# Attention key rests of four heads in one score unit, and a new place for the turns of q, k and X

## The chip, the cores and the metric

One core of a Trainium2 chip runs the whole program. The metric is the time of one execution on the device, in microseconds; smaller is better. The kernel before takes 453.09 us (median of 3 runs, 452.95 to 453.27). The profiled execution has a span of 451.7 us, and all times inside it are counted from the start of that span.

The engines are named as in the profile: PE is TensorE (matmuls), PEld its weight loads, DVE is VectorE, ACT is ScalarE, POOL is GpSimd, SP is SyncE, which here only issues transfers.

## The reference, cut to what matters

```python
def _attn_ref(q, k, v):                      # (8, 12, 448, 64) each: batch, heads, sequence, head width
    scores = (1.0 / np.sqrt(64)) * np.matmul(q, k.transpose(0, 1, 3, 2))
    attn = softmax(scores)                   # over the keys
    return np.matmul(attn, v)

def reference(q, k, v, w_gate, w_val, w_out):
    x = attn_out.transpose(0, 2, 1, 3).reshape(8 * 448, 768)
    g = x @ w_gate                           # 768 x 1536
    val = x @ w_val                          # 768 x 1536
    return (g * sigmoid(g) * val) @ w_out    # 1536 x 768
```

There are 96 heads, which the kernel takes in 48 pairs (two heads of 64 columns fill 128 partitions), six pairs for each of the eight batch entries. The FFN works on eight blocks of 384 or 512 rows of x.

## The kernel before

The parts that the change touches. A pair goes through these steps: q and k are loaded and turned (transposed) to `qkT`; `qk` makes the scores of one group of 112 keys for both heads and ScalarE takes the exponential; `pv_chunk` multiplies the exponentials with the values and with a column of ones, so that the sum of the softmax comes out as column 64; VectorE divides; `turn_x` turns the result into `X`, the moving operand of the FFN.

```python
NPE = 11       # pairs 1 to 10 have q and k turned by TensorE, later ones by a transposing DMA
XPE = 12       # pairs 0 to 11 have X turned by TensorE
FIRST = 6      # pairs worked on before the first FFN step
# ...
    ps_s = ctx.enter_context(tc.tile_pool(name="ps_s", bufs=3, space=PSUM))   # 3 x 2 banks
    ps_f = ctx.enter_context(tc.tile_pool(name="ps_f", bufs=2, space=PSUM))   # 2 banks
# ... in prep(pr), for pairs 1 to 10:
        def turn():
            if pr < FIRST + 2:
                tp = ps_s.tile([128, 2, 1024], FP16, tag="s", name="tp")[:, 0]
            else:
                tp = ps_f.tile([128, 1024], FP16, tag="f", name="tp")
            for i in range(2 * NC + 1):
                t, c = (1 - i // NC, i % NC) if i < 2 * NC else (0, 0)
                for hx in range(2):
                    src = raw[pr][t][:, hx, c, :]
                    nc.tensor.transpose(tp[ts(hx, 64), ts(i, P)], src, ident[0:P, 0:P])
            nc.vector.tensor_copy(qkT[pr][:], tp[:, 0 : 2 * S + D])
# ...
    def qk(pr, c):                                    # c = 0..3: 112 keys each
        t = qkT[pr]
        s = ps_s.tile([128, 2, 512], FP32, tag="s")
        for hx in range(2):
            nc.tensor.matmul(
                s[:, hx, 0:S],
                lhsT=t[ts(hx, 64), c * P : c * P + 128],
                rhs=t[ts(hx, 64), ds(S + (1 - hx) * D, S)],
                start=True, stop=True,
            )
        e = Es[pr % NE][:, ds(c * EB, 16)].rearrange("p (h b) x -> p h (b x)", h=2)
        nc.scalar.activation(e[:, :, 0:S], s[0:P, :, 0:S], AF.Exp, scale=sm_scale)
# ...
    def pv_chunk(pr, c):                              # 8 matmuls of 65 columns; 4 chunks a pair
        if c == 0:
            accs[pr] = ps_f.tile([128, 512], FP32, tag="f", name="acc")      # one bank a pair
        # ... six matmuls of 128 queries of one head, two of the last 64 queries of both heads
        if c < NC - 1:
            return
        nc.vector.reciprocal(r[:, 0:7], a7[:, :, D])
        nc.vector.tensor_tensor(xt[:, 0:n], a7[:, 0:n, 0:D],
                                r[:, 0:n].unsqueeze(2).to_broadcast([128, n, D]), ALU.mult)
# ...
    def turn_x(pr):
        if pr < XPE:
            tp = accs[pr] if pr < FIRST else ps_f.tile([128, 512], FP32, tag="f", name="xtp")
            for j in range(3):
                nc.tensor.matmul(tp[:, ts(j, 128)], lhsT=xt[:, 2 * j : 2 * j + 2].rearrange("p h d -> p (h d)"),
                                 rhs=ident[:], start=True, stop=True)
            nc.vector.tensor_copy(dst[:, 0:MQ], tp[:, 0:MQ])
            return
        # ... else two transposing DMAs
    # turn_rests(b): the last 64 queries of six pairs, 12 matmuls of 64 columns
```

After a start of six pairs the program goes in visits. A visit has two or three score units, up to two products of earlier pairs, and then its share of the first FFN (`gp` and `vp`, six matmuls each) and of the second (`op`, twelve matmuls). The end of a visit in `before`:

```python
            for _, p0 in todo:
                pv(p0)
                if p0 < XPE:
                    turns.append(p0)
                else:
                    turn_x(p0)
            # ... the visit's FFN steps: run_fv(), run_o() ...
            if x == 1:
                turn_rests(0)
            while turns:
                turn_x(turns.pop(0))
```

In the second FFN `op` comes from `ps_f`, ScalarE brings it to `osb`, and the rows are stored. The last 128 rows of all are treated apart, so that their second half is evacuated and stored in two quarters of 192 columns:

```python
        for ch, oh in steps:
            last = last_block and ch == n // 128 - 1
            # ...
            parts = [(oh * OH, OH)]
            if last and oh:
                parts = [(OH, OH // 2), (OH + OH // 2, OH // 2)]
```

Of the kernel before, what the change touches and what calls it, by code (L numbers as in the profile page):

```python
# [19 lines left out]
NPE = 11  # L20
# [3 lines left out]
WIDE = 8  # L24
XPE = 12
NE = 4
NX = 6
NV = 5
VS = 9
EB = 15  # L30
# [3 lines left out]
def kernel(  # L34
# [24 lines left out]
    MQ = S - D  # L59
# [13 lines left out]
    load_table("exp_and_others")  # L73

# [7 lines left out]
    ps_f = ctx.enter_context(tc.tile_pool(name="ps_f", bufs=2, space=PSUM))  # L82

    Es = [consts.tile([P, NC * EB + 1, D], FP16, name=f"E{i}") for i in range(NE)]
    Xts = [consts.tile([128, 7, D], FP16, name=f"xt{i}") for i in range(NX)]
    Xrs = [consts.tile([D, 128], FP16, name=f"xr{i}") for i in range(3)]
    Vts = [consts.tile([P, 2, NC, D + 2], FP16, name=f"vo{i}") for i in range(NV)]
    vraw = consts.tile([P, VS, 2, NC, D], FP16, name="vraw")
# [11 lines left out]
    wo = [consts.tile([128, NFB, OH], FP16, name=f"wo{i}") for i in range(2)]  # L100
# [5 lines left out]
    def dummy(n):  # L106
        wp = ps_f.tile([128, 512], FP32, tag="f", name="wp")
        for _ in range(n):
            nc.tensor.matmul(wp[:], lhsT=warm[:, 0:128], rhs=warm[:], start=True, stop=True)  # L109

    def load_qk32(pr):
        rq = raws.tile([P, 2, NC, D], FP32, tag="rq", bufs=RB)
        rk = raws.tile([P, 2, NC, D], FP32, tag="rk", bufs=RB)
        for dst, src in ((rq, q), (rk, k)):
            nc.sync.dma_start(dst[:], src[0, 2 * pr : 2 * pr + 2].rearrange("h (p c) d -> p h (c d)", c=NC))
        raw[pr] = (rq[:], rk[:])
# [3 lines left out]
    def load_qk16(pr, n=2):  # L120
        h0 = 2 * (pr % 2) if pr >= 14 else 0
        if h0 == 0:
            q16 = raws.tile([P, 4, NC, D], FP16, tag="rq", bufs=RB, name="q16")
            k16 = raws.tile([P, 4, NC, D], FP16, tag="rk", bufs=RB, name="k16")
            pairbuf[:] = [q16, k16]
        q16, k16 = pairbuf
        for dst, src in ((q16, q), (k16, k)):
            flat = src.rearrange("b h s d -> (b h) s d")[2 * pr : 2 * pr + 2 * n]
            nc.gpsimd.dma_start(dst[:, ds(h0, 2 * n)], flat.rearrange("h (p c) d -> p h (c d)", c=NC))  # L129
        for i in range(n):  # L130
            h = h0 + 2 * i
            raw[pr + i] = (q16[:, h : h + 2], k16[:, h : h + 2])

    def load_v(pr, n=1):
        b, h = divmod(2 * pr, H)
        nc.gpsimd.dma_start(  # L136
            vraw[:, ds(pr % VS, n)].rearrange("p r h c d -> p (r h) (c d)"),
            v[b, h : h + 2 * n].rearrange("h (p c) d -> p h (c d)", c=NC),
        )
# [4 lines left out]
    def load_w(kind, i):  # L144
        if kind == "o":
            src = moe_w_out[:, ts(i, OH)].rearrange("(f p) m -> p f m", p=128)
            dst = wo[i]
        else:
            src = (moe_w_gate if kind == "g" else moe_w_val)[:, ts(i, DF // 4)].rearrange(
                "(t a p) m -> t p a m", p=128, t=2  # L150
            )
            for t in range(2):
                nc.gpsimd.dma_start(wgv[kind, i][:, ts(t, NCB // 2), :], src[t])
            return
        nc.gpsimd.dma_start(dst[:], src)

    def prep(pr):
        rq, rk = raw[pr]
        if pr == 0 or pr >= NPE:
            qk16 = attp.tile([P, 2, NC, 2, D], FP16, tag="qk16", bufs=3)  # L160
            for t, src in enumerate((rq, rk)):
                dst = qk16[:, 1 - t].rearrange("p c h d -> p h c d")
                if pr == 0:
                    nc.vector.tensor_copy(dst[:, 0], src[:, 0])
                    nc.scalar.activation(dst[:, 1], src[:, 1], AF.Copy)
                else:
                    nc.gpsimd.tensor_copy(dst, src)  # L167
        qkT[pr] = attp.tile([128, 2 * S + D], FP16, tag="qkT", name="qkT", bufs=5)
        if pr >= NPE:
            nc.sync.dma_start_transpose(  # L170
                qkT[pr][:, 0 : 2 * S].rearrange("p (c q) -> p c q", q=P),
                qk16[:].rearrange("p t c h d -> p (t c h d)"),
            )
            nc.sync.dma_start_transpose(
                qkT[pr][:, 2 * S :].rearrange("p (c q) -> p c q", c=1),
                qk16[0:D, 1, 0].rearrange("p h d -> p (h d)"),
            )
            return None

        def turn0():  # L180
            for t in range(2):
                tp = ps_s.tile([128, 2, 512], FP32, tag="s", name="tp")
                for c in range(NC):
                    for hx in range(2):
                        nc.tensor.matmul(
                            tp[ts(hx, 64), c // 2, ds(c % 2 * P, P)],
                            lhsT=qk16[:, 1 - t, c, hx],
                            rhs=ident[0:P, 0:P],
                            start=True,
                            stop=True,  # L190
                        )
                dst = qkT[pr][:, ts(1 - t, S)].rearrange("p (a x) -> p a x", a=2)
                nc.vector.tensor_copy(dst[:, 0], tp[:, 0, 0 : 2 * P])
                nc.scalar.activation(dst[:, 1], tp[:, 1, 0 : 2 * P], AF.Copy)
                if t == 0:
                    tq = tp
            nc.vector.tensor_copy(qkT[pr][:, 2 * S :], tq[:, 0, 0:D])

        def turn():
            if pr < FIRST + 2:  # L200
                tp = ps_s.tile([128, 2, 1024], FP16, tag="s", name="tp")[:, 0]
            else:
                tp = ps_f.tile([128, 1024], FP16, tag="f", name="tp")
            for i in range(2 * NC + 1):
                t, c = (1 - i // NC, i % NC) if i < 2 * NC else (0, 0)
                for hx in range(2):
                    src = raw[pr][t][:, hx, c, :]
                    nc.tensor.transpose(tp[ts(hx, 64), ts(i, P)], src, ident[0:P, 0:P])  # L208
            nc.vector.tensor_copy(qkT[pr][:], tp[:, 0 : 2 * S + D])  # L209

        return turn if pr else turn0

    def qk(pr, c):
        t = qkT[pr]
        s = ps_s.tile([128, 2, 512], FP32, tag="s")
        for hx in range(2):
            nc.tensor.matmul(  # L217
                s[:, hx, 0:S],
                lhsT=t[ts(hx, 64), c * P : c * P + 128],
                rhs=t[ts(hx, 64), ds(S + (1 - hx) * D, S)],  # L220
                start=True,
                stop=True,
            )
        e = Es[pr % NE][:, ds(c * EB, 16)].rearrange("p (h b) x -> p h (b x)", h=2)
        nc.scalar.activation(e[:, :, 0:S], s[0:P, :, 0:S], AF.Exp, scale=sm_scale)  # L225

    def qk_half(pr, half, between=None):
        for c in (2 * half, 2 * half + 1):
            qk(pr, c)
            if between and c % 2 == 0:  # L230
                between()
# [3 lines left out]
    def pv_chunk(pr, c):  # L235
        if c == 0:
            accs[pr] = ps_f.tile([128, 512], FP32, tag="f", name="acc")
        e = Es[pr % NE]
        vo = Vts[pr % NV]
        a7 = accs[pr][:, 0 : 7 * (D + 1)].rearrange("p (s d) -> p s d", s=7)  # L240
        for j in range(3):
            for hx in range(2):
                nc.tensor.matmul(  # L243
                    a7[:, 2 * j + hx],
                    lhsT=e[:, ds(c * EB + 9 * hx + 2 * j, 2)].rearrange("p b x -> p (b x)"),
                    rhs=vo[:, hx, c, 0 : D + 1],
                    start=c + j + hx == 0,
                    stop=False,
                )
        for hx in range(2):  # L250
            nc.tensor.matmul(  # L251
                a7[:, 6],
                lhsT=e[:, ds(c * EB + 6 + hx, 2)].rearrange("p b x -> p (b x)"),
                rhs=vo[:, hx, c, 0 : D + 1],
                start=False,
                stop=c == NC - 1 and hx == 1,
            )
        if c < NC - 1:
            return
        r = attp.tile([128, 8], FP32, tag="R", bufs=2, name="R")  # L260
        xt = Xts[pr % NX]
        nc.vector.reciprocal(r[:, 0:7], a7[:, :, D])  # L262
        n = 7 if pr < XPE else 6
        nc.vector.tensor_tensor(  # L264
            xt[:, 0:n],
            a7[:, 0:n, 0:D],
            r[:, 0:n].unsqueeze(2).to_broadcast([128, n, D]),
            ALU.mult,
# [373 lines left out]
```

The softmax here doesn't subtract the row's maximum and nothing guards it: scores larger than these inputs give would overflow.

## Time and profile before

| | us |
|---|---|
| median time of 3 runs | 453.09 |
| span of the profiled execution | 451.7 |
| exponentials on ACT, 192 | 162.1 busy, 919 ns each |
| products of both kinds on PE, 1536 matmuls | 53.0 and 42.9 busy |
| scores on PE, 384 matmuls | 50.6 busy |
| first FFN on PE, 1152 matmuls | 124.7 and 124.6 busy |
| second FFN on PE, 684 matmuls | 116.1 busy |
| first FFN step of the first block starts at | 29.8 |
| last FFN block's first step starts at | 393.8 |

Matmuls overlap in their pipeline, and the recorded length of one counts its whole way through the array. So the busy times of the groups add up to more than the engine's own, and the price of a matmul is better read from the distance between two starts. The granted clock of TensorE is full in all 40 slices of the profile.

In a timeline a line gives the start, the length, the engine, the line of the kernel, the operation, what it writes and reads, its shape, how many are merged, and in brackets how long the engine was idle before it and who released it.

### The profile page before, as it was taken

To read this page: it belongs to the slowest core of one execution; us is meant where nothing else is said; L and a number is where in the kernel's file an instruction comes from. 1 tells how busy PE (TensorE), PEld (TensorE's weight loads), DVE (VectorE), ACT (ScalarE), POOL (GpSimd) and SP (SyncE) were. 2 spreads that over 40 slices of the span, in tenths; PEclk is the share of its full clock that TensorE was granted. 3 is DMA by queue.
4 is the path that set the end of the run, shared out by engine and by line. 5 is a ranking of instruction groups with operands and counts; after the bars stand their busy time and mean duration, and the time that the engine had idled before them with its cause. 6 is when DMAs were issued, how large, how long until landed. Compare 5 with 4: busy or idle time off the path is not lost.

```text
span 451.7 us, 9871 instructions
## 1 busy us (share of the span) xinstructions
PE 441.9 (98%) x4024; PEld 247.0 (55%) x4024; DVE 201.6 (45%) x447; ACT 238.8 (53%) x350; POOL 141.8 (31%) x228
## 2 busy tenths in 40 slices
PE   8999999999999999999999999999999999999995
PEld 3655565545455556454555656545455666544563
DVE  3666562456654434455443534353453544055300
ACT  6965666566746465554554546644555462222221
POOL 8755715927642225252313405330100000000000
PEclk9999999999999999999999999999999999999999
DMA  9999999999969379874749758772503112200033
GB/s 142 173 200 201 196 172 174 180 209 119 145 93 133 46 129 124 132 120 71 126 74 120 98 78 143 118 105 68 101 20 68 46 46 57 70 2 0 17 100 95
DMA packets 105101, 48.71 MB, mean 108 GB/s; under 512 B 59744, under 2 KB 101600, under 8 KB 105056
## 3 DMA queue, kind: packets, MB, share of 16 engines
q0 software_dynamic: 43392, 23.37, 41.2%
q1 hardware_dynamic: 61664, 24.71, 28.9%
q8 instruction: 31, 0.51, 0.5%
q14 instruction: 14, 0.11, 0.1%
HBM read 47.19 MB, written 11.01 MB: 129 GB/s over the span
## 4 chain that ended last, share of the span: by engine, by line
PE 93%; DVE 3%; ACT 2%; issue 1%; DVEq 0%; ACTq 0%
PE op L371 24%; PE gp L326 23%; PE vp L326 23%; PE s L217 9%; PE acc L243 9%; PE acc L251 2%; ACT E L225 2%; PE tp L208 1%; PE wp L109 1%; DVE t L345 1%; ACT sg L341 1%; DVE qkT L209 0%; DVE xt L264 0%; PE acc L291 0%; DVE hts L348 0%
## 5 line engine op out<-in xcount | busy, mean ns | idle before, releaser
L225 ACT ACTIVATE E<-s 112x896 f16<-112x896 f32 x192 | 162.1, 919 | 27.5 <-PE s L217 27.4
L326 PE MATMUL gp<-X,wg 128*128 128x384 f16 (+1 forms) x576 | 124.7, 352 | 0.0
L326 PE MATMUL vp<-X,wv 128*128 128x384 f16 (+1 forms) x576 | 124.6, 352 | 0.0
L371 PE MATMUL op<-wo,hts 128*128 128x384 f16 (+1 forms) x684 | 116.1, 323 | 0.0
L345 DVE SCALAR_TENSOR_TENSOR t<-sg,gp 128x384 f32<-128x384 f32 (+1 forms) x96 | 59.7, 621 | 121.8 <-ACT sg L341 121.8
L341 ACT ACTIVATE sg<-gp 128x384 f32<-128x384 f32 (+1 forms) x96 | 52.5, 547 | 84.8 <-PE gp L326 83.6
L371 PEld LDWEIGHTS <-hts 128*128 128x128 f16 x684 | 65.5, 98 | 45.9 <-issue 3.9
L326 PEld LDWEIGHTS <-wv 128*128 128x128 f16 x576 | 56.3, 98 | 52.6
L326 PEld LDWEIGHTS <-wg 128*128 128x128 f16 x576 | 53.1, 97 | 45.6 <-issue 1.1
L378 ACT ACTIVATE osb<-op 128x384 f32<-128x384 f32 (+1 forms) x57 | 27.8, 487 | 92.5 <-PE op L371 92.5
L167 POOL COPY qk<-q 112x512 f16<-112x512 f16 x37 | 22.9, 619 | 144.5 <-DMA qkT<-qk 143.1
L348 DVE SCALAR_TENSOR_TENSOR hts<-t,vp 128x384 f16<-128x384 f32 (+1 forms) x96 | 59.6, 621 | 10.0
L243 PEld LDWEIGHTS <-E 112*128 112x128 f16 x1152 | 46.7, 97 | 18.2 <-issue 17.5
L243 PE MATMUL acc<-vo,E 112*128 112x65 f16 x1152 | 53.0, 193 | 1.3 <-DVE vo L142 0.7
L217 PE MATMUL s<-qkT 64*128 64x448 f16 x384 | 50.6, 355 | 0.2
L251 PE MATMUL acc<-vo,E 112*128 112x65 f16 x384 | 42.9, 193 | 0.0
L262 DVE RECIPROCAL R<-acc 128x7 f32<-128x7 f32 x48 | 9.8, 205 | 70.6 <-PE acc L251 70.5
L129 POOL DMA_DIRECT2D k<-in_k_dram x44 | 29.0, 660 | 9.5 <-DMA wo<-in_moe_w_out_dram 7.8
L129 POOL DMA_DIRECT2D q<-in_q_dram x44 | 29.3, 666 | 5.2 <-PE s L217 2.5
L136 POOL DMA_DIRECT2D vraw<-in_v_dram x42 | 28.0, 666 | 8.4 <-DVE vo L142 7.2
L217 PEld LDWEIGHTS <-qkT 64*128 64x128 f16 x384 | 14.5, 94 | 25.8 <-issue 18.6
L264 DVE TENSOR_TENSOR xt<-acc,R 128x384 f16<-128x384 f32 (+1 forms) x48 | 27.6, 574 | 1.7
(41 smaller groups left out, 148.2 us busy)
## 6 DMA issues: line engine op xcount, KB each, us to landing
q<-in_q_dram POOLq DMA_DIRECT2D x41, 112.0 KB, 4.0
k<-in_k_dram POOLq DMA_DIRECT2D x41, 112.0 KB, 4.6
vraw<-in_v_dram POOLq DMA_DIRECT2D x39, 112.0 KB, 4.6
wg<-in_moe_w_gate_dram POOLq DMA_DIRECT2D x8, 288.0 KB, 10.1
wv<-in_moe_w_val_dram POOLq DMA_DIRECT2D x8, 288.0 KB, 10.2
wo<-in_moe_w_out_dram POOLq DMA_DIRECT2D x2, 1152.0 KB, 22.0
out_dram<-osb SPq DMA_DIRECT2D x8, 288.0 KB, 3.0
out_dram<-osb SPq DMA_DIRECT2D x8, 240.0 KB, 3.1
```

Of the source, the lines that this page charges most:

```text
L129: nc.gpsimd.dma_start(dst[:, ds(h0, 2 * n)], flat.rearrange("h (p c) d -> p h (c d)", c=NC))
L136: nc.gpsimd.dma_start(vraw[:, ds(pr % VS, n)].rearrange("p r h c d -> p (r h) (c d)"), v[b, h : h + 2 * n].rearrange("h (p c) d -> p h (c ...
L217: nc.tensor.matmul(s[:, hx, 0:S], lhsT=t[ts(hx, 64), c * P : c * P + 128], rhs=t[ts(hx, 64), ds(S + (1 - hx) * D, S)], start=True, stop=True,)
L225: nc.scalar.activation(e[:, :, 0:S], s[0:P, :, 0:S], AF.Exp, scale=sm_scale)
L243: nc.tensor.matmul(a7[:, 2 * j + hx], lhsT=e[:, ds(c * EB + 9 * hx + 2 * j, 2)].rearrange("p b x -> p (b x)"), rhs=vo[:, hx, c, 0 : D + 1] ...
L251: nc.tensor.matmul(a7[:, 6], lhsT=e[:, ds(c * EB + 6 + hx, 2)].rearrange("p b x -> p (b x)"), rhs=vo[:, hx, c, 0 : D + 1], start=False, st ...
L326: nc.tensor.matmul(dst[:, 0:n], lhsT=wslice(kind, fb, cb), rhs=X[kk][:, cb, ds(c0, n)], start=(cb == 0), stop=(cb == NCB - 1),)
L341: nc.scalar.activation(sg[:, 0:n], gp[:, 0:n], AF.Tanh, scale=0.5)
L345: nc.vector.scalar_tensor_tensor(t1[:, 0:n], sg[:, 0:n], 1.0, gp[:, 0:n], ALU.add, ALU.mult)
L348: nc.vector.scalar_tensor_tensor(hts[:, fb, 0:n], t1[:, 0:n], 0.5 * HS, vp[:, 0:n], ALU.mult, ALU.mult)
L371: nc.tensor.matmul(op[:, 0:w], lhsT=hts[:, fb, ts(ch, 128)], rhs=wo[oh][:, fb, ds(m0 - oh * OH, w)], start=(fb == 0), stop=(fb == NFB - 1),)
L378: nc.scalar.activation(osb[:, ds(m0, w)], op[:, 0:w], AF.Copy, scale=1.0 / HS)
```

## The change

Three things are changed, and much follows from them.

**Key rests shared by four heads.** The 448 keys of a head are taken as three groups of 128 and a rest of 64, instead of four groups of 112. The rests of two heads of each of two neighbouring pairs make one score unit: four matmuls of 64 x 64 tiles, two above each other in one PSUM tile. So two pairs have seven units and seven exponentials, where they had eight. To have the rows at the right partitions, values, and the keys of the pairs that the DMA turns, are loaded in two halves of 64 partitions; the key in the middle of each seven is loaded into both.

**More turns by TensorE.** `NPE` goes from 11 to 14 and `XPE` from 12 to 18. The turn of X now takes all 448 queries of a pair at once, so `turn_rests` goes away.

**Order.** The start follows a written list (`START`), and the turns move: in visits with no product the turn of q and k comes behind the first FFN step; in visits with one, the turns come before the FFN steps.

```diff
-NPE = 11
+NPE = 14
-XPE = 12
+XPE = 18
-NX = 6
+NX = 3
+NR = 3
...
     def qk(pr, c):
-        t = qkT[pr]
         s = ps_s.tile([128, 2, 512], FP32, tag="s")
-        for hx in range(2):
-            nc.tensor.matmul(
-                s[:, hx, 0:S],
-                lhsT=t[ts(hx, 64), c * P : c * P + 128],
-                rhs=t[ts(hx, 64), ds(S + (1 - hx) * D, S)],
...
+        if c < KR:
+            t = qkT[pr]
+            for hx in range(2):
+                nc.tensor.matmul(
+                    s[:, hx, 0:S],
+                    lhsT=t[ts(hx, 64), ts(c + low(pr, hx), 128)],
+                    rhs=t[ts(hx, 64), ds(NC * 128, S)],
...
+        else:
+            for hx in range(2):
+                for p in (pr, pr + 1):
+                    lo = low(p, hx)
+                    t = qkT[p]
+                    nc.tensor.matmul(
+                        s[ts(1 - lo, 64), hx, 0:S],
+                        lhsT=t[ts(hx, 64), ds(0 if lo else KR * 128 + 64, 64)],
+                        rhs=t[ts(hx, 64), ds(NC * 128, S)],
...
+    def pv_open(pr):
+        if pr not in accs:
+            if wide(pr):                     # pairs 0 to 5 and the last two
...
+            else:
+                accs[pr] = ([fbank(), fbank()], [0, 0])
+
+    def pv_close(pr):
...
+        for hx in range(2):
+            a4 = accs[pr][0][hx][:, 0 : (KR + 1) * (D + 1)].rearrange("p (s d) -> p s d", s=KR + 1)
+            r = attp.tile([128, KR + 1], FP32, tag="R", bufs=4, name="R")
+            nc.vector.reciprocal(r[:], a4[:, :, D])
+            nc.vector.tensor_tensor(
+                xt[:, :, hx],
+                a4[:, :, 0:D],
+                r[:].unsqueeze(2).to_broadcast([128, KR + 1, D]),
+                ALU.mult,
             )
 
-    def pv(pr):
-        for c in range(NC):
-            pv_chunk(pr, c)
+    def pv(pr, mid):
+        for hx in range(2):
+            for c in range(KR):
+                pv_piece(pr, c, (hx,))
+            if hx == 0:
+                mid()
+        pv_close(pr)
...
         if pr < XPE:
-            tp = accs[pr] if pr < FIRST else ps_f.tile([128, 512], FP32, tag="f", name="xtp")
-            for j in range(3):
+            tp = ps_s.tile([128, 2, 512], FP32, tag="s", name="xtp")[:, 0]
+            for j in range(KR + 1):
+                n = min(128, S - j * 128)
...
                 while l < l0 + 128:                              # second FFN, the stores
                     b, j = divmod(l, S)
-                    c, p0 = divmod((j + D) % S, P)
-                    m = min(P - p0, l0 + 128 - l, (MQ if j < MQ else S) - j)
+                    n = S // NC
+                    c, p0 = divmod(j, n)
+                    m = min(n - p0, l0 + 128 - l)
...
             for _, p0 in todo:
-                pv(p0)
+                pv(p0, run_turns)
                 if p0 < XPE:
                     turns.append(p0)
                 else:
...
+            def between():
+                run_turns()
+                if x + 7 < NPE:
+                    prep(x + 7)()
+
+            if not bare:
+                between()
+            if steps:
+                nf, no = steps.pop(0)
...
+                gate_small[0] = bare
                 for y in range(nf):
-                    if fvq:
-                        run_fv()
+                    run_fv()
+                    if bare and y == 0:
+                        between()
                 for _ in range(no):
                     run_o()
-            if x == 1:
-                turn_rests(0)
-            while turns:
-                turn_x(turns.pop(0))
```

A visit now has three score units in every case but the first (whose two already stand in the start's list) and the last, and at most one product. The eight rest matmuls of a product (`pv_piece(p0, RU)`) come directly behind the visit's scores. The second FFN of the first block moves from its own visits to those of the second block. `w_out` is loaded in four pieces instead of two, later.

## Prediction

> **What bounds the kernel now.** I read the page's busy table first, then the chain that ended last, then TensorE's timeline in a settled stretch and in the two places where it waits.
>
> ```profile
> PE 441.9 (98%) x4024; PEld 247.0 (55%) x4024; DVE 201.6 (45%) x447; ACT 238.8 (53%) x350; POOL 141.8 (31%) x228
> PE 93%; DVE 3%; ACT 2%; issue 1%; DVEq 0%; ACTq 0%
> ```
>
> TensorE is busy for 441.9 of 451.7 us and the chain of work is 93% TensorE. All else is half idle. So time is won by taking TensorE work away, and lost wherever TensorE waits inside its own order of instructions; ScalarE time matters only in the start, where 26 exponentials of 0.84 us stand close together between 6.6 and 29.3 us.
>
> TensorE's timeline of one settled stretch (start us, length us, what, count) gives the price of each kind of work:
>
> ```profile
> 157.63 0.74 PE L217 MATMUL s<-qkT 64*128 64x448 f16 x6
> 158.31 0.35 PE L243 MATMUL acc<-vo,E 112*128 112x65 f16 x6
> ...
> 159.28 1.14 PE L326 MATMUL gp<-X,wg 128*128 128x384 f16 x6
> 160.26 1.14 PE L326 MATMUL vp<-X,wv 128*128 128x384 f16 x6
> 161.23 2.11 PE L371 MATMUL op<-wo,hts 128*128 128x384 f16 x12
> 163.28 0.74 PE L217 MATMUL s<-qkT 64*128 64x448 f16 x6
> 163.95 0.34 PE L371 MATMUL op<-wo,hts 128*128 128x384 f16 x1
> ```
>
> Read start to start. Twelve second-FFN matmuls take 1.95 us, 162.5 ns each. The next scores start 0.10 us after them (161.23 + 1.95 = 163.18, start 163.28). Three score units (two heads each) take 0.67 us; two took 0.48 us in another visit (33.78 to 34.26), so one unit is 0.19 us and a batch pays 0.10 us on each side. The product of one pair with its values (32 matmuls) takes 159.28 - 158.31 = 0.97 us, 30.3 ns each.
>
> Two other rows are needed: two column halves at work together, and the one place where TensorE waits for a softmax division.
>
> ```profile
> 37.15 0.38 PE L310 MATMUL rtp<-ident,xt 128*64 128x64 f16 x12 [0.19 <-DVE t L345]
> 37.46 0.55 PE L217 MATMUL s<-qkT 64*128 64x448 f16 x4
> ```
>
> Twelve matmuls of 64 columns, alternating between two halves of the array, fill 0.38 us; a single one lasts 0.197 us, so 11 steps took 0.18 us, 16.6 ns each.
>
> ```profile
> 28.43 0.22 PE L251 MATMUL acc<-vo,E 112*128 112x65 f16 x2
> 28.68 0.21 DVE L262 RECIPROCAL R<-acc 128x7 f32<-128x7 f32 x1 [0.17 <-PE acc L251]
> 28.93 0.63 DVE L264 TENSOR_TENSOR xt<-acc,R 128x448 f16<-128x448 f32 x1
> 29.61 0.34 PE L291 MATMUL acc<-ident,xt 128*128 128x128 f16 x3 [0.96 <-DVE xt L264]
> ```
>
> When the turn of X follows its own product with nothing between, TensorE idles 0.96 us behind reciprocal and multiplication. Counted from where the next matmul could have started (28.43 + 2 x 0.030 = 28.49) it loses 1.12 us. Before, this happens at the end of the start only; later, X is turned at the end of a visit, after the FFN steps.
>
> **What the Trainium skill says.** "TensorEngine Tiling (Array Packing)", Key Properties: a change of tiling mode drains TensorE, while tiles of one mode run independently. The trace agrees: 0.10 us on each side of a batch of half-height scores, and 16.6 ns per matmul for two halves. "PSUM — Partial Sum Buffer", Engine vs sequencer instructions: matmuls start and complete in program order, only weight loads are pulled ahead. The trace agrees at 29.61 us, where FFN matmuls ready to run stay behind the waiting turn. "TensorE: Matmul & The Clock Gate", Back-to-back issue gap: N/2.4 + 2.5 ns; 384 columns give 162.5 ns, exactly the row above.
>
> **The change, part by part.** The FFN stays at 327 us (576 x 162.5 ns, 576 x 216 ns, 56 x 1.95 us).
>
> A. Scores. 192 units become 168: three of 128 keys per pair and one rest unit per two pairs. After the start, before has 168 units in 58 batches: 168 x 0.19 + 58 x 0.20 = 43.5 us. After has 145 in 49 batches: 27.6 + 9.8 = 37.4 us; in 21 batches the rest unit (64 x 64 tiles) stands beside whole ones and adds a mode change of 0.10, 2.1 us. This holds if the four rest matmuls share the array. Saved: 4.0 us.
>
> B. Products. The 8 rest matmuls of a pair use half the rows each and alternate. At 16.6 ns instead of 30.3 a pair costs 24 x 30.3 + 8 x 16.6 = 0.86 us instead of 0.97. 42 pairs after the start: 4.6 us saved.
>
> C. Turns of q and k by TensorE. In the visits pairs 7 to 13 instead of 8 to 10. One was 0.57 us (34.26 to 34.83) and about 0.1 of switching, three make 2.0 us. One is now 16 small (16.6 ns), 8 of 112 columns (25 ns) and three mode changes, 0.27 + 0.20 + 0.30 = 0.77 us, seven make 5.4 us. Added: 3.4 us.
>
> D. Turns of X. Six of 0.18 us and two rest turns of 0.4, 1.9 us, become twelve of 0.21 us (pairs 6 to 17): 2.5 us. Added: 0.6 us.
>
> E. The start. 23 exponentials stand before the first FFN step instead of 26, which is 2.5 us of ScalarE. TensorE has about 20 us of work there, so it becomes nearly the limit itself, with only one accumulator. I take 2 us saved.
>
> So far this is 8.6 us of saving in A and B, 4.0 spent in C and D, 2 more saved: 6.6 us faster, near 446.5.
>
> F. Where X's turn stands. In a visit with a product, after.py puts the pair into `turns` after `pv`, and `between()` empties that list directly after, ahead of the FFN step. The hook in the middle of `pv` always finds an empty list. Twelve times the turn thus follows its own division at once. The two heads are closed one after the other, each from its own bank. Twelve matmuls (0.36 us) lie between the end of head 0 and of head 1. From the rows of 128x384 (557 ns) and 128x448 (625 ns) a multiplication of 256 columns is 0.42 us. With T the end of head 1: head 0's reciprocal (0.20) and multiplication start at T - 0.32 and end, with 0.03 between instructions, at T + 0.33; head 1's follow and end at T + 1.01; the turn starts at T + 1.06. T lies 0.16 after the place where the next matmul could have started, so each costs 1.22 us. Twelve: 14.6 us.
>
> G. Both FFN banks. The product now holds both banks of the pool it shares with the second FFN operand and the second FFN. Where a visit ends with a first-FFN step, VectorE must finish `hts` first: 0.9 us after the step's last matmul, against the 0.77 us that three scores give. About 11 visits, some 0.2 us each: 2 us.
>
> H. The end. The inner loop of the second FFN now assigns `n = S // NC`, so `last` is never true again: the last rows are not halved. The last evacuation is 0.49 us instead of 0.33, and the last store is 336 KB (4.2 us to landing in the table of transfers) instead of 48 KB (2.0 us). About 2 us.
>
> Sum: -6.6 + 14.6 + 2 + 2 = +12 us, 465. Before already idles 2.7 us between 29.8 and 86.6 us (56.8 us long, 54.1 us of work by the prices above), some of which the new waits will cover, and E and H are rough. I choose 463.
>
> **Rivals.** (1) The saving wins: if VectorE's chain were hidden, about 449 with G and H. For it speak the 98% and the fewer instructions; against it the order itself, in which nothing stands between product and turn. (2) The rest units gain nothing, because their four matmuls run two at a time (21 x 0.19 = 4 us more) and rest products stay at 30 ns (4.6 us more): about 471. Against it speak the 16.6 ns of the two column halves; no row of before shows four quarters at work. (3) Loads become the bound: GpSimd issues keys and values in two halves (0.66 us an issue, some 76 more, 50 us), with a seventh of the rows read twice. GpSimd is busy only 31%, and in before the last gate and value weights are issued at 38.8 us and land within 11.8 us, well ahead of need. A late load in the start could cost 2 to 3 us, about 466.
>
> **Range and chances.** The work left for TensorE cannot give 2%: even with E in full and none of F, G, H the time stays near 446, above the 444.0 that this needs. Faster by over 2%: 0.03. The border to slower by over 2% is 462.2. F is the large term, 12 waits of 1.0 to 1.3 us; with 1.0, and the savings somewhat better, 457 comes out; with rival 2 in part, 469. Hence 454 to 469, within 2%: 0.40, slower: 0.57.
>
> **What would show it.** TensorE's matmuls `xtp<-ident,xt` waiting for `xt` some 12 us in all in the table of waits, 12 times, right after a product; score units of 0.19 us including the rest unit; 0.86 us from the first rest product to the next kind of work; the first FFN step near 27.5 us; about 7 us instead of 5 between the last matmul and the end. I am wrong if those waits are short, if FFN steps lie between product and turn, or if a TensorE wait on a transfer appears.

## Result and the profile after

| | before | after |
|---|---|---|
| median time, us | 453.18 | 466.66 |
| lowest to highest | 452.95 to 454.66 | 466.41 to 468.08 |
| span of the profiled execution | 451.7 | 464.8 |
| first FFN step starts at | 29.79 | 26.62 |
| first step of the last FFN block starts at | 393.8 | 407.0 |

The changed kernel is slower: ratio 1.0297, 95% interval 1.0267 to 1.0327. The predicted time was 463.0, the range 454 to 469.

The busy table and the chain of work of the changed kernel, to be set beside those of before:

```profile
PE 441.9 (95%) x4163; PEld 248.1 (53%) x4163; DVE 206.5 (44%) x464; ACT 219.9 (47%) x325; POOL 178.7 (38%) x298
PE 87%; DVE 6%; ACT 5%; issue 1%; DVEq 0%; ACTq 0%
```

TensorE is busy for exactly as long as before, 441.9 us, in a span that is 13.1 us longer. ScalarE lost 19 us of work and nothing came of it. In the chain the share of TensorE falls from 93% to 87%, VectorE takes 6% instead of 3% and ScalarE 5% instead of 2%: the chain now passes through divisions, copies and exponentials for which TensorE stands still. The equal busy times do not say that no work was saved: the recorded length of a matmul runs on into the wait behind it, so a wait of 1.08 us from start to start shows as 0.92 us of idle time, and most of the short waits below show as none.

The table of waits of the changed kernel (engine, line, what it waited for, us in total, times, the longest):

```profile
PEld L364 <- DVE xt L337: 12.5, 12, 1.0
PE xtp L364 <- DVE xt L337: 8.3, 9, 0.9
PE s L256 <- DVE qkT L247: 2.3, 2, 1.2
PE f L291 <- DVE hts L410: 1.2, 6, 0.2
```

The first row is the one to read: the weight load of X's turn waits for the division, 12 times and 12.5 us in all. The second row has nine of the same waits again on the matmul side; in the three others the exponential on the PSUM slot ended 0.04 to 0.05 us later by this profile, and the wait is put down to it. Rows three and four are two smaller waits.

One visit of the changed kernel, its timeline without weight loads and GpSimd:

```profile
46.73 0.74 PE L256 MATMUL s<-qkT 64*128 64x448 f16 x6
47.04 0.55 DVE L410 SCALAR_TENSOR_TENSOR hts<-t,f 128x384 f16<-128x384 f32 x1
47.14 2.54 ACT L277 ACTIVATE E<-s 128x896 f16<-128x896 f32 x3 [0.79 <-PE s L256]
47.31 0.19 PE L291 MATMUL f<-vo,er 64*128 64x65 f16 x1
47.52 0.29 DVE L168 COPY vo<-vraw 128x512 f16<-128x512 f16 x1
47.65 0.28 PE L291 MATMUL f<-vo,er 64*128 64x65 f16 x7
47.86 0.91 PE L291 MATMUL f<-vo,E 128*128 128x65 f16 x24
48.44 0.18 DVE L336 RECIPROCAL R<-f 128x4 f32<-128x4 f32 x1 [0.64 <-PE f L291]
48.66 0.42 DVE L337 TENSOR_TENSOR xt<-f,R 128x256 f16<-128x256 f32 x1
49.00 0.17 DVE L336 RECIPROCAL R<-f 128x4 f32<-128x4 f32 x1
49.21 0.42 DVE L337 TENSOR_TENSOR xt<-f,R 128x256 f16<-128x256 f32 x1
49.69 0.37 PE L364 MATMUL xtp<-ident,xt 128*128 128x128 f16 x4 [0.92 <-ACT E L277]
```

The product's 24 full matmuls start at 47.86 and need 0.73 us; the turn starts at 49.69, 1.83 us later. Between them VectorE does four instructions, head 0 and then head 1, as the prediction drew it. In the last line the wait is put down to an exponential, which ended at 49.68; the second multiply ended at 49.63, so without the exponential the turn would have started 0.05 us earlier at most. And at the top, one of the eight rest matmuls runs at 47.31 and the other seven start 0.34 us later, when `hts` has ended at 47.59: the second FFN bank was not free.

The start-to-start distances between the first FFN step and the last FFN block, summed by the kind of matmul that opens each stretch (a wait is counted with the kind in front of it):

| us | before | after | of it waits |
|---|---|---|---|
| scores | 38.80 | 34.87 | 3.1 |
| rest products | - | 14.28 | 5.4 |
| products | 40.88 | 44.09 | 13.0 |
| turns of q and k | 1.70 | 4.80 | |
| turns of X | 2.68 | 2.86 | |
| first FFN, gate | 93.52 | 93.56 | |
| first FFN, value | 96.08 | 95.38 | |
| second FFN | 90.34 | 90.53 | |
| sum | 364.00 | 380.37 | 21.5 |

Without its waits the changed kernel would do scores and products in 71.7 us where before takes 79.7. The two kinds have to be taken together: the switch from half-height to full-height matmuls stands behind the scores in before and behind the rest products in the changed kernel.

### The profile page after: what moved, and what is told of

Its sections match the earlier page's. It is cut to its first block, busy times and chain, and to the rows that moved or that the text cites. A ratio compares the mean times of both kernels' runs of the same rounds, so it can differ in the third digit from the quotient of the medians.

```text
span 464.8 us, 10196 instructions
## 1 busy us (share of the span) xinstructions
PE 441.9 (95%) x4163; PEld 248.1 (53%) x4163; DVE 206.5 (44%) x464; ACT 219.9 (47%) x325; POOL 178.7 (38%) x298
## 3 DMA queue, kind: packets, MB, share of 16 engines
q1 hardware_dynamic: 54800, 23.06, 26.8%
## 4 chain that ended last, share of the span: by engine, by line
PE 87%; DVE 6%; ACT 5%; issue 1%; DVEq 0%; ACTq 0%
PE f L433 24%; PE f L388 23%; PE gp L388 21%; PE f L291 8%; PE s L256 5%; ACT E L277 3%; DVE xt L337 2%; PE s L269 2%; PE acc L291 1%; DVE t L407 1%; DVE hts L410 1%; ACT sg L403 1%; PE xtp L364 1%; PE tp L246 1%; PE wp L117 1%
## 5 line engine op out<-in xcount | busy, mean ns | idle before, releaser
L277 ACT ACTIVATE E<-s 128x896 f16<-128x896 f32 x144 | 123.1, 924 | 11.8 <-PE s L256 11.5
L388 PE MATMUL f<-X,wv 128*128 128x384 f16 (+1 forms) x576 | 124.6, 352 | 0.0
L433 PE MATMUL f<-wo,hts 128*128 128x384 f16 x672 | 115.5, 326 | 0.0
L388 PE MATMUL gp<-X,wg 128*128 128x512 f16 (+1 forms) x522 | 113.5, 354 | 0.0
L440 ACT ACTIVATE osb<-f 128x384 f32<-128x384 f32 x56 | 27.5, 491 | 107.0 <-PE f L433 102.8
L410 DVE SCALAR_TENSOR_TENSOR hts<-t,f 128x384 f16<-128x384 f32 (+1 forms) x96 | 59.6, 621 | 10.0
L124 POOL DMA_DIRECT2D vraw<-in_v_dram x82 | 51.1, 653 | 3.9 <-DVE hts L410 1.2
L291 PEld LDWEIGHTS <-E 128*128 128x128 f16 x1152 | 37.8, 97 | 3.9 <-issue 1.2
L291 PE MATMUL f<-vo,E 128*128 128x65 f16 x960 | 36.2, 193 | 0.0
L337 DVE TENSOR_TENSOR xt<-f,R 128x256 f16<-128x256 f32 x80 | 34.0, 424 | 2.8
```

What stands on the lines that cost most here:

```text
L124: eng.dma_start(dst[ts(s, 64)], rows)
L277: nc.scalar.activation(e[:, 0 : 2 * S].rearrange("p (h q) -> p h q", h=2), s[:, :, 0:S], AF.Exp, scale=sm_scale)
L291: nc.tensor.matmul(accs[pr][0][hx][:, ts(j, D + 1)], lhsT=e[rows, ds(hx * S + j * 128, 128)], rhs=Vts[pr % NV][rows, hx, col, 0 : D + 1], ...
L337: nc.vector.tensor_tensor(xt[:, :, hx], a4[:, :, 0:D], r[:].unsqueeze(2).to_broadcast([128, KR + 1, D]), ALU.mult,)
L388: nc.tensor.matmul(dst[:, 0:n], lhsT=wslice(kind, fb, cb), rhs=X[kk][:, cb, ds(c0, n)], start=(cb == 0), stop=(cb == NCB - 1),)
L410: nc.vector.scalar_tensor_tensor(hts[:, fb, 0:n], t1[:, 0:n], 0.5 * HS, vp[:, 0:n], ALU.mult, ALU.mult)
```

## Experiments

**1. X turned in the next visit.** The theory: the twelve waits behind the division are the loss. The rival: TensorE would wait a little later for the same engines.

```diff
             def between():
-                run_turns()
+                if bare:
+                    run_turns()
```

> After, with the turn of X of pairs 6 to 17 moved out of its own visit: it runs in the middle of the next visit's product, or behind the first FFN step where the next visit has no product. Nothing else changes. Theory (the twelve waits of 1.09 us behind the division are the loss): the rows xtp<-ident,xt no longer wait for xt, 13 us less minus 0.1 us each for the PSUM slot of the first score unit, so about 454.5. Rival (TensorE would wait for the same things a little later, in the FFN step, because ScalarE and VectorE are behind): under 4 us less, 463 or more.

Measured: 455.76 us, ratio to before 1.0051 (1.0032 to 1.0069). TensorE's timeline of this run, the same visit:

```profile
45.97 0.54 PE L291 MATMUL f<-vo,E 128*128 128x65 f16 x12
46.35 0.36 PE L364 MATMUL xtp<-ident,xt 128*128 128x128 f16 x4
46.55 0.53 PE L291 MATMUL f<-vo,E 128*128 128x65 f16 x12
```

The turn now stands between the two heads of the next product, and 0.38 us after the first 12 matmuls it runs, with no wait. In the sums by kind the products fall from 44.09 to 32.98 us. The median is 10.9 us under that of the changed kernel, and the span of the profiled execution 11.1 us, where the waits were 13.0: they are gone, but a product with the turn in its middle takes 0.80 to 0.89 us in eight visits and 1.15 and 1.21 us in two, against 0.74 us for one without, and so 1.9 us come back. The rival falls.

**2. The same wait put into the kernel before.** If the placement alone does it, before must show it too.

```diff
                 pv(p0)
-                if p0 < XPE:
-                    turns.append(p0)
-                else:
-                    turn_x(p0)
+                turn_x(p0)
```

> Before, with one thing of the change done alone: X of pairs 6 to 11 is turned directly behind its own product instead of at the end of the visit. Theory: six waits of 0.96 us idle, 1.12 us from start to start, so 6.7 us more, about 459.8. Rival (before has slack elsewhere that takes the wait in): under 2 us more.

Measured: 459.35 us, ratio 1.0127 (1.0095 to 1.0159), 5.7 us more than the 453.64 of before, measured beside it. Its timeline and its table of waits:

```profile
38.61 0.22 PE L251 MATMUL acc<-vo,E 112*128 112x65 f16 x2
39.78 0.34 PE L291 MATMUL xtp<-ident,xt 128*128 128x128 f16 x3 [0.96 <-DVE xt L264]
39.97 1.14 PE L326 MATMUL gp<-X,wg 128*128 128x384 f16 x6
```

```profile
PE xtp L291 <- DVE xt L264: 5.7, 6, 1.0
```

Six turns, six waits of 0.96 us idle. The wait does not need the rest units or the two banks; it comes from the place alone. In the sums by kind the products take 6.8 us more, as expected; the turns of X take 1.0 us less, which is why the time grows by 5.7 and not by 6.7 us.

**3. The turn of q and k before the FFN step everywhere.** Two waits that the prediction did not have: scores wait for the copy of `qkT`. TensorE and VectorE in the changed kernel:

```profile
33.09 0.44 PE L246 MATMUL tp<-ident,k 64*64 64x64 f16 x16
33.78 0.55 PE L256 MATMUL s<-qkT 64*128 64x448 f16 x4
34.28 0.56 DVE L410 SCALAR_TENSOR_TENSOR hts<-t,f 128x384 f16<-128x384 f32 x1
34.75 0.65 DVE L247 COPY qkT<-tp 128x960 f16<-128x960 f16 x1
35.45 0.36 PE L256 MATMUL s<-qkT 64*128 64x448 f16 x2 [1.13 <-DVE qkT L247]
```

Behind the FFN step the turn stands directly before the next visit's scores. Its copy comes after `hts` on VectorE, and the third score unit reads it.

```diff
-            if not bare:
-                between()
+            between()
...
                 for y in range(nf):
                     run_fv()
-                    if bare and y == 0:
-                        between()
```

> After, with the turn of q and k placed before the first FFN step in the visits without a product too. Theory (scores wait 0.5, 1.29 and 1.31 us for the copy of qkT at 29.4, 33.8 and 62.3 us, because the turn now stands directly before the scores that read it): these waits go, 3 us less, about 463.5. Rival (the placement was right, the copy of qkT would then delay hts and the FFN step): no change or up to 1 us more.

Measured: 465.29 us, ratio 1.0247 (1.0215 to 1.0279). The rows for `qkT` leave the table of waits, and the median falls by 1.4 us of the 3 expected. Between the first FFN step and the last block 2.3 us are saved: the scores take 2.2 us less and the rest products 0.6 us more, and one turn of 0.7 us now stands in front of the first FFN step and so outside this stretch. That step starts 1.2 us later than in the changed kernel's profile, 0.8 us for the turn and 0.4 us because in this profile the whole start runs later (first scores at 6.74 instead of 6.32). The theory names the wait rightly, and less than half of its size comes out.

**4. The last 128 rows.** Step H of the prediction said that the lost halving costs 2 us.

```diff
-                    n = S // NC
-                    c, p0 = divmod(j, n)
-                    m = min(n - p0, l0 + 128 - l)
+                    rows_ = S // NC
+                    c, p0 = divmod(j, rows_)
+                    m = min(rows_ - p0, l0 + 128 - l)
```

> After, with the inner variable of the store loop given another name, so that the last 128 rows are again evacuated and stored in two quarters at the end. The prediction's step H says 2 us less (464.7). Rival: the end after the last matmul is as long in after (5.25 us from the last start to the end of the span) as in before (5.28), so the size of the last store costs nothing there: under 0.5 us of change.

Measured: 465.27 us, ratio 1.025 (1.0221 to 1.0278). From the first matmul of the last second-FFN stretch to the end of the span it takes 25.1 us, against 26.7 in the changed kernel: 1.6 us less. So here the halving is worth nearly what H said. But the same distance in before, which has the halving, is 26.8 us: the rival's premise (two ends of equal length) is as true as H's gain. The traces show what differs. Before stores each of the last quarters as 64 rows and 64 rows, all issued by SyncE, which takes 0.55 to 0.60 us for each of these issues. The last evacuation ends at 446.92, the last store is issued 1.3 us later, at 448.26, and lands at 450.26. In this run the quarters go out as 112 rows from SyncE and 16 from ScalarE; the last two are issued at 460.94 and 460.95, right after the evacuation's end at 460.92, and have landed at 462.86. This is read from the traces; a version of before with its stores on two engines was not run.

**5. The three edits together.**

> After with three edits together: X turned in the next visit, the turn of q and k before the first FFN step in all visits, the last 128 rows stored in two quarters. Theory (the three causes lie one after the other on TensorE's path and add up): 455.8 with the first alone, 1.1 less and 1.6 less by the spans of the other two, so 453, level with before (ratio 0.998 to 1.002). Rival (they overlap, or the moved turns get in each other's way): 455 or more.

Measured: 454.5 us, ratio 1.003 (1.0014 to 1.0047), between the two expectations. TensorE's timeline and the table of waits show a wait that had not been seen before, but for 0.17 us in experiment 1:

```profile
68.75 0.55 PE L256 MATMUL s<-qkT 64*128 64x448 f16 x4
71.32 0.36 PE L256 MATMUL s<-qkT 64*128 64x448 f16 x2 [2.01 <-DMA qkT<-qk]
```

```profile
PE s L256 <- DMA qkT<-qk: 2.0, 1, 2.0
PE xtp L364 <- ACT er L277: 1.1, 2, 0.6
```

With the waits gone TensorE arrives earlier than the first `qkT` that the transposing DMA makes, which lands at 71.18 us. In the changed kernel it landed at 69.93, and the same scores ran at 76.01 only: the waits for the division had covered this transfer. And X's turn in front of the FFN step waits 0.56 us for its PSUM slot.

**6. X by the transposing DMA.** Would it not be simplest to leave these turns to the DMA, as before does from pair 12?

```diff
-XPE = 18
+XPE = 6
```
(on top of the edits of 3 and 4; with XPE = 6 the edit of 1 has no turn left to move)

> After with the turn of q and k before the FFN step and the last rows in two quarters, and with X of pairs 6 to 17 turned by the transposing DMA (XPE = 6) instead of TensorE. Theory (each turn of X by TensorE costs 1.09 us of waiting and 0.2 us of work): twelve turns less, 15.5 us less than after with the same two edits (464), so 448.5 to 451. Rival (TensorE's turns were there because the transposing DMA comes too late while the weights are loading): FFN steps wait for X, 455 or more.

Measured: 465.54 us, ratio 1.0261 (1.0247 to 1.0275). The rival holds. The table of waits:

```profile
PE gp L388 <- DMA X<-xt: 7.4, 2, 3.7
PE s L256 <- DVE vo L168: 4.5, 1, 4.5
```

Two FFN steps wait 3.7 us each for a transposed X. The 4.5 us of the second row stand before the scores that waited in experiment 5. The row names a value copy, but scores do not read values; the transposed `qkT` of this pair lands at 71.94 and the scores start at 72.08, the same 0.14 us later as in experiment 5 (71.18 and 71.32). So it is the transposing DMA there too. So at this stage the turns by TensorE do have a use; only their place was bad.

**7. Pairs 12 and 13 by the DMA again**, on top of the three edits (`NPE = 12`).

> The three edits, with pairs 12 and 13 turned by the transposing DMA again (NPE = 12). Theory (a turn of q and k costs TensorE 0.7 us and nothing is won): 1.4 us less than the three edits. Rival (the transposing DMA is late at this place, with the weights under way): scores wait on a transfer for qkT and it takes 1 us or more longer.

Measured: 458.64 us, ratio 1.0099 (1.0078 to 1.012), 4.1 us more than the three edits. TensorE's timeline:

```profile
58.29 0.56 PE L256 MATMUL s<-qkT 64*128 64x448 f16 x4 [1.47 <-DMA qkT<-qk]
71.66 0.56 PE L256 MATMUL s<-qkT 64*128 64x448 f16 x2 [3.22 <-DMA qkT<-qk]
```

4.7 us of waiting for two transposed `qkT`, where the profile of the three edits has 2.0, against 1.5 us of turns saved. This part of the change is right for this stage.

**8. Rest products between the heads**, on top of the three edits, where the visit before ended with a first-FFN step.

```diff
             if hx == 0:
                 mid()
+                if late:
+                    pv_piece(pr, RU)
```

> The three edits, and in visits that follow a first-FFN step the eight rest matmuls of the product stand between the two heads instead of in front of both. Theory (in some 13 visits the rest matmuls wait 0.2 to 0.4 us for the FFN bank that hts still reads, because they need both banks at once): those waits go, 0.35 us each, for 0.1 us more of mode change, so 3 us less than the three edits alone. Rival (the wait only moves to the next user of the banks): within 1 us of the three edits.

Measured: 455.05 us, ratio 1.0034 (1.002 to 1.0048), no gain. The rest products fall from 14.64 to 10.22 us in the sums by kind, so the wait for `hts` is what stood in them. But products rise by 1.9, scores by 1.35 and turns of X by 0.6 us: half-height and full-height matmuls now alternate more often (the 12 matmuls in front of the rest products take 0.47 instead of 0.38 us), the scores have the switch behind them again, and the turn of X comes earlier and waits five times for its PSUM slot, 0.8 us in all. Nearly all is given back.

**9. w_out later**, on top of the three edits.

```diff
-            9: [("o", 0), ("o", 1)],
-            11: [("o", 2), ("o", 3)],
+            12: [("o", 0)],
+            13: [("o", 1)],
+            14: [("o", 2)],
+            15: [("o", 3)],
```

> The three edits, with the four pieces of w_out loaded when pairs 12, 13, 14 and 15 are entered instead of two each at 9 and 11. Theory (with the waits gone TensorE reaches the scores of the first pair turned by the transposing DMA before its qkT has landed, a 2.0 us wait at 71.3 us, and that landing is slow because 2.3 MB of w_out stand before it): the wait goes, 2 us less than the three edits, about 452.5. Rival (the loads of q and k themselves are late): the wait stays, 454.5.

Measured: 453.67 us, ratio 1.0003 (0.9995 to 1.0011). At the place of the 2.01 us wait TensorE's timeline now reads:

```profile
68.65 0.74 PE L256 MATMUL s<-qkT 64*128 64x448 f16 x6
69.23 0.19 PE L291 MATMUL f<-vo,er 64*128 64x65 f16 x1
```

The wait is gone. The two transfers of this pair land in 4.5 and 5.2 us, where they took 8.7 and 11.0 us in experiment 5; they are also issued 1.5 to 2 us earlier. So it was the load of w_out beside them. The median gains 0.8 us where 2 were expected; the three edits' profiled execution, with its 2.0 us, was one of the longer ones of that kernel (457.1 against a median of 454.5), so the wait was probably smaller in most.

**10. X behind the FFN step again in visits with no product**, on top of 9.

> As the one with w_out later, and in visits with no product the turn of X stands behind the first FFN step again (only the turn of q and k stays in front). Theory (in front it waits 0.56 us for an exponential to free its PSUM slot, in three visits): 1 us to 1.5 us less than the one with w_out later, about 451.3, under before by 0.5%. Rival: the slot wait only moves to the next FFN step, no change.

Measured: 453.1 us, ratio 0.9991 (0.9976 to 1.0005): 0.6 us less, level with before. The 1.1 us of waiting for an exponential leave X's turn; a turn of q and k in front of an FFN step keeps two waits of 0.55 us, and the scores behind the FFN step get a new one of 0.7 us. So part of the wait has only moved, as the rival said, and half of the gain expected comes out.

**11. XPE = 12**, on top of 10.

> As the one with X behind the FFN step, with X of pairs 12 to 17 turned by the transposing DMA (XPE = 12). Theory (in time, now that w_out no longer loads at 60 us but still loads at 80 to 100): six turns of 0.2 to 0.3 us less, about 450. Rival (w_out now collides with these transposes): FFN steps wait for X, 453 or more.

Measured: 451.14 us, ratio 0.9949 (0.9937 to 0.9961): under both kernels. Its table of waits has no row of TensorE waiting for a transfer of X or of `qkT`. The turns of X cost 1.28 us instead of 2.45 in the sums, and the products 31.84 instead of 33.02. Pairs 12 to 17 reach the FFN late enough for the DMA; pairs 6 to 11 did not in experiment 6, with w_out in its first place, and were not tried with w_out later.

It is worth a look where the 2.3 us come from by which its profiled span is shorter than that of before: 2.2 from the start, 1.2 from the end, while between the first FFN step and the last block it takes 1.1 us more than before (365.2 against 364.0). Scores, rest products and products together take 80.0 us there, against 79.7 in before. So the work saved by the shared rests is still eaten by waits, nearly 6 us of them in front of or between the rest products, and experiment 8, which took most of them out, lost as much elsewhere.

**12. The same with NPE = 12.**

> The fastest version so far (three edits, w_out later, X behind the FFN step in visits with no product, XPE = 12), with pairs 12 and 13 turned by the transposing DMA (NPE = 12). Theory (these turns were late beside w_out only): 1.4 us of TensorE less, 449.7. Rival (their own loads are late, since they are issued behind the gate and value weights at about 46 us): scores wait for qkT near 58 us and at the next pairs, no gain or up to 3 us more, 451 to 454.

Measured: 452.25 us (449.43 to 461.47 in 22 executions), ratio 0.9979 (0.9963 to 0.9994). The ratio is that of the 19 executions up to 455.39 us and leaves out three slower ones. The median lies in the rival's range, 1.1 us above experiment 11, and only the best execution reaches the theory's number; the 19 alone spread over 6 us, ten times as far as the five of experiment 11. In its profile TensorE waits 1.0 us before scores at 58.9, whose `qkT` lands at 58.76 (by this profile an exponential ends 0.07 us later and gets the wait), 1.2 us at 96.7 behind a division that itself waits for a transfer of X, 0.9 us for w_out and 0.2 for another `qkT`. So transfers are late again in this execution; that they make the spread is likely, not shown.

## Why the prediction was right

Each step against what the profile and the runs show, in us of change:

| step | predicted | measured | from |
|---|---|---|---|
| A, B scores and products | -8.6 | -8.0 | sums by kind, waits taken out |
| C turns of q and k | +3.4 | +3.1 | sums by kind |
| D turns of X | +0.6 | +0.2 | sums by kind |
| E start | -2 | -3.2 | first FFN step, 29.79 to 26.62; see below |
| F X behind its division | +14.6 | +13.0 | 12 x 1.08 |
| G both FFN banks | +2 | +5.4 | rest products over 0.21 each |
| H end | +2 | -0.2 | 26.82 and 26.66 from the last stretch |
| FFN steps | 0 | -0.4 | sums by kind |
| not in the sum: scores behind the turn | 0 | +3.1 | 0.5, 1.29 and 1.31 |
| sum | +12 | +13.0 | span, 451.7 to 464.8 |

From its sum of +12, 465, the prediction went down to 463, because some idle time of before would be covered by the new waits. That hardly happened (-0.4 in the FFN steps); the measured median is 466.66.

The mechanism was right: TensorE bounds the kernel, the structure takes 8 us of work from it, of which the added turns take 3.3 back, and the place of X's turn puts 13 us of standing still in. Experiments 1 and 2 show that from both sides.

A and B: eight rest products and 24 full ones take 0.96 us to the FFN step behind them where nothing waits (145.07 to 146.03), which is the predicted 0.86 and one switch of 0.10.

F's chain of four VectorE instructions came out in the order drawn, 0.18 and 0.42 us each, and the first starts where it was put, 0.33 us before the end of head 1. 1.22 us was 0.14 too much, mostly because the second reciprocal starts 0.08 us before the first multiplication has ended (49.00, and 48.66 + 0.42 = 49.08), where the prediction put a gap of 0.03; the shorter reciprocals (0.18, not 0.20) are the rest.

G was too small. The prediction counted 11 visits of 0.2 us. In the profile ten visits lose 0.34 or 0.39, three 0.21, and 15 more, which come behind a second-FFN step, lose 0.06 to 0.12 each; what these 15 wait for was not looked into. The batch of scores that was to cover the wait is also shorter than assumed: 0.58 us from its first matmul to the first rest matmul, where the prediction's prices give 0.67. That fits the 0.10 us of a switch which falls away, since rest products have the same half height as the scores.

H failed as a difference between the two kernels. The end after the start of the last matmul did not grow from 5 to 7 us: it is 5.42 us in before and 5.37 in the changed kernel. The last large store landed in 2.8 us, not in the 4.2 of before's table, and what experiment 4 gains by halving, before loses in the queue of SyncE.

The missing term is the copy of `qkT` before the scores. The program's order had the turn directly in front of the scores that read it; the prediction looked for divisions only. E was about right. The same start puts the first FFN step at 26.62, 26.95 and 27.45 us in three profiles (the changed kernel's and those of experiments 1 and 4), so 2.3 to 3.2 us are saved; TensorE does 23 score units and 24 product pieces there in 20.3 us, of which 0.95 are idle.

G and the missing term together are 6.5 us too low, F, H and E 5.0 too high in this profile, so part of the closeness is luck.

Of the rivals, (1) fell with the order, but it was too hopeful as well: with VectorE's chain hidden the kernel takes 455.8 us (experiment 1), not 449, since the waits of G and for `qkT` remain. (2) fell: four rest matmuls of 448 columns take 0.31 us with one mode change in it (40.74 to 41.05), so 0.21, nearly what one whole unit needs (0.19). (3) fell for the changed kernel as it stands, and came up as soon as the waits were taken away (experiments 5 to 7): the first transposed `qkT` lands at nearly the same time in the changed kernel and in experiment 5 (69.93 and 71.18 us), while TensorE comes to it some 7 us earlier.

## What to carry to other kernels

When an engine with one order of instructions is the limit, look at every place where it consumes what another engine makes from its own last result, and put independent work of at least that chain's length in between; here 1.1 us twelve times undid a structural saving of 8 us. Small waits on a shared buffer count too: 5.4 us of them, none over 0.4 us, were the part that stayed to the end. Before a stall is taken out, look at which transfers it covers: they are the next wait, and the order of loads has to be tuned again together with it. An empty hook is worth a look: here the right place for the turn was already in the code, but the list was always emptied before it was reached.

## What was not expected of the hardware

Rest products, half the rows high and alternating between the two halves, take 0.21 us for eight with the switch to full height in it (127.36 to 127.57); without the 0.10 us of the switch that is about 0.11 us, or 14 ns each, against 30.3 ns for the full-height ones of the same 65 columns.

A transposing DMA for `qkT` lands in 4.3 us in the middle (run of experiment 5), but up to 11.0 us while weights load. In experiments 5 to 7 one late transfer of this kind cost TensorE 1.5 to 4.5 us at a stretch, more than a product of 0.74 us with its turn of 0.2.
